# Second MoE of an attention + MoE + MoE kernel: the down side as seven block products, after a block's whole up side

## The chip, the cores and the metric

The kernel runs on one core of a Trainium2 chip. The core has five engines that the texts name as the profile does: PE (TensorE, matmuls; PEld is its weight loads), DVE (VectorE), ACT (ScalarE), POOL (GpSimd) and SP (SyncE, which here issues nearly all DMAs). Each engine runs its own instructions in order and waits on semaphores that the others raise. The metric is the device time of one execution in microseconds, lower is better.

## The reference

Attention with a memory term gives x of 2304 tokens x 512; two MoE-like layers follow, and only the second is touched here (cut to what matters):

```python
def _moe2_ref(x, w_gate, w_val, w_out):        # x 2304x512, d_ff 1536
    g = x @ w_gate
    silu = g * (1.0 / (1.0 + np.exp(-g)))
    val = x @ w_val
    return (silu * val @ w_out).astype(np.float32)

def reference(**kwargs):
    ...
    attn_out = _attn_ref(**attn_kwargs)
    x = attn_out.transpose(0, 2, 1, 3).reshape(B * S, H * D)
    x = _moe_ref(x=x, **moe_kwargs)            # the same without w_val, d_ff 2048
    return _moe2_ref(x=x, **moe2_kwargs)
```

All is float32. The kernel computes each float32 product as three products of a high and a low half (high x high, low x high, high x low) in the float32r format, so every logical matmul is three on PE.

## The kernel before, in words

One program, three stages that overlap. Attention and the first MoE run mixed: a generator (moe1) hands out pieces of the first MoE, and the main loop puts attention steps between them by a table of goals; Tile's scheduler then orders each engine by a model of times. The first MoE works in segments of 256 or 320 tokens: h = x W_in (line 824), tanh on ACT, a product on DVE, the halves gh on ACT and gl on POOL (line 834), y = g W_out (line 883). Its result goes to DRAM (yd).

**Preparing the second MoE's weights** (prep_w2) runs step by step beside that: a step every third yield of moe1 in attention (every=3), every fourth later (late=4). Per f-tile j (12 of 128 columns of d_ff) it loads and decodes the gate, value and down weights in turn, forms on POOL the sums that Strassen's products need of gate and value (S), splits all into halves (high on ACT, low on POOL) and writes them to DRAM, four tiles a j for the up side (wd2) and one for the down side (wdo, or directly the resident wos). By the end of the first MoE all is prepared; the down weights of all 12 f-tiles lie in SBUF (wos).

**The second MoE** takes 3 blocks i of 768 tokens. The up side computes gate and value of one f-tile for both halves of a block (384 tokens each) by Strassen's seven products in Winograd's form instead of eight: up(i, j) issues seven groups of six matmuls of 384 columns (2 pieces of the contraction x 3 halves) into four kinds of PSUM banks: a (product A11, later A12), c (S1), b (copied from a by ACT, then S2, S3, A22 on top) and d (added by DVE from b and c, then S4). Seven names of y (B11, T1, T2, B21, T3, B22, T4) are the sums of tokens that y_prep forms. Then tanh (ACT) and three DVE operations give the gated result r of each half.

The down side is a plain product: split_p splits a result r into ph (ACT, line 1174) and pl (POOL, line 1175); down adds, per f-tile and half, three token tiles x three matmuls of 512 columns into three resident banks po; after the twelfth f-tile ACT scales a bank into ot and SP writes it out. These nine matmuls are cut into three units, and up puts them between its own products: the down side of one half follows results that exist already, and the last half of the last block remains for the end.

In the second MoE the order of PE is the written one (manual_schedule); the other engines are ordered by the scheduler. stream() loads the four weight tiles of an f-tile one f-tile ahead, through eight buffers. y_prep of the next block runs at j = 8 to 11. The lines that make the chain between PE and the helpers:

```python
        nc.scalar.copy(b, a)                    # 1144
        product(b, "S2", "T2", False)
        d = seeded("d")
        nc.vector.tensor_add(d, b, e)           # 1147
```

## Time and profile before

| | before |
|---|---|
| three timed runs | 1105.01 us median (1103.02 to 1108.28) |
| the profiled execution's own time | 1105.75 us |
| its span on the core | 1103.9 us |
| PE busy / weight loads busy | 1070.8 us (97%) / 967.4 us (88%) |
| DVE, ACT, POOL busy | 609.2, 524.8, 453.2 us |
| DMA | 224.6 MB, 203 GB/s in the mean |
| chain that ended last | PE 77%, DVE 8%, DMA 7%, ACT 3%, POOL 3% |
| PE's share of that chain by line | 824: 14%, 1189: 14%, 883: 13%, 1120: 24% in all |

Busy time of PE counts the time in which at least one matmul is in flight, and the next one begins before the last one ends, so 97% does not say how dense the matmuls follow each other: that is read from starts. A row of a timeline merges neighbouring instructions of one kind: its start, how long it took from first start to last end, and, in brackets, the idle time of its engine before it and who ended it.

### The profile page before, as it was taken

The numbers are of one execution on the slowest core, as the hardware profiler recorded it, in microseconds if no ns is written. First come the engines' busy times: TensorE is split into PE (matmuls) and PEld (weight loads), VectorE is DVE, ScalarE is ACT, GpSimd is POOL, SyncE is SP. The second block draws the span as 40 slices with busy tenths as digits, with TensorE's granted clock in tenths as the row PEclk, the third lists the DMA queues.
The fourth block names the chain that finished last, engine by engine and source line by source line (L and its number), as shares of the span: only waits on it lengthen the run. The fifth ranks groups of instructions, "written<-read, shape, count | busy, mean of one in ns | idle before, by whom it ended". The sixth has DMA issues, their size and how long they took to land.

```text
span 1103.9 us, 19308 instructions
## 1 busy us (share of the span) xinstructions
PE 1070.8 (97%) x6899; PEld 967.4 (88%) x6899; DVE 609.2 (55%) x1412; ACT 524.8 (48%) x1261; POOL 453.2 (41%) x529
## 2 busy tenths in 40 slices
PE   7889999999999999999999999999999999999998
PEld 4566888888899889988899999999899999999986
DVE  6997588986566656466744564333643333333320
ACT  6665587765666465556644442222522323323222
POOL 3676446576666455656434831001211111121122
PEclk8987999999999999999999999999999999999999
DMA  8876576565688566785459866666654554655501
GB/s 212 280 213 208 158 241 207 155 206 172 216 286 268 198 193 212 274 293 182 150 209 391 287 251 228 202 194 192 237 183 159 182 172 142 201 162 177 175 20 49
DMA packets 155344, 224.64 MB, mean 203 GB/s; under 512 B 75632, under 2 KB 108400, under 8 KB 155248
## 3 DMA queue, kind: packets, MB, share of 16 engines
q1 hardware_dynamic: 153072, 223.00, 62.1%
q8 instruction: 55, 0.90, 0.3%
q10 hardware_dynamic: 2176, 0.40, 0.2%
q14 instruction: 41, 0.34, 0.1%
HBM read 169.88 MB, written 53.48 MB: 202 GB/s over the span
## 4 chain that ended last, share of the span: by engine, by line
PE 77%; DVE 8%; DMA 7%; ACT 3%; POOL 3%; issue 2%; SPq 0%; POOLq 0%; ACTq 0%; DVEq 0%
PE h L824 14%; PE po L1189 14%; PE y L883 13%; PE gb L1120 10%; PE ga L1120 7%; PE gd L1120 3%; PE gc L1120 3%; PE pss L403 3%; PE U L588 3%; PE pst L336 3%; DMA raw<-in_moe_w_out_dram 2%; DMA raw<-in_moe_w_val_dram 2%; DVE t L701 1%; PE psm L414 1%; PE pss L478 1%
## 5 line engine op out<-in xcount | busy, mean ns | idle before, releaser
L1175 POOL TENSOR_TENSOR pl<-r,ph 128x384 fp32r<-128x384 f32 x72 | 75.1, 1051 | 343.4 <-ACT ph L1174 282.2
L883 PE MATMUL y<-gh,w 128*128 128x320 f32 (+1 forms) x1024 | 175.2, 305 | 1.8 <-DVE th L832 1.5
L824 PE MATMUL h<-xh,w 128*128 128x320 f32 (+1 forms) x1024 | 171.3, 306 | 5.4 <-ACT w L209 2.3
L834 POOL TENSOR_TENSOR gl<-th,gh 128x256 fp32r<-128x256 f32 (+1 forms) x128 | 112.3, 881 | 131.2 <-ACT gh L209 97.0
L824 PEld LDWEIGHTS h<-xh,w 128*128 128x128 f32 x1024 | 146.1, 192 | 13.7 <-ACT w L209 3.7
L883 PEld LDWEIGHTS y<-gh,w 128*128 128x128 f32 x1024 | 146.8, 190 | 7.9 <-DVE th L832 2.5
L1189 PE MATMUL po<-wo,ph 128*128 128x512 f32 x432 | 133.8, 395 | 1.1 <-ACT ph L1174 0.7
L1120 PE MATMUL gb<-yT,w 128*128 128x384 f32 x648 | 131.7, 338 | 2.8 <-ACT gb L1144 1.4
L1120 PEld LDWEIGHTS gb<-yT,w 128*128 128x128 f32 x648 | 116.1, 188 | 12.7 <-ACT gb L1144 2.1
L1147 DVE TENSOR_TENSOR gd<-gb,e 128x384 f32<-128x384 f32 x36 | 20.4, 565 | 145.5 <-PE gb L1120 142.4
L832 DVE SCALAR_TENSOR_TENSOR th<-th,h 128x256 f32<-128x256 f32 (+1 forms) x128 | 56.9, 450 | 73.3 <-ACT th L831 73.0
L883 PE MATMUL y<-gl,w 128*128 128x320 f32 (+1 forms) x512 | 94.4, 300 | 0.2 <-POOL gl L834 0.2
L824 PE MATMUL h<-xl,w 128*128 128x320 f32 (+1 forms) x512 | 93.1, 301 | 0.0
L1189 PEld LDWEIGHTS po<-wo,ph 128*128 128x128 f32 x432 | 79.2, 188 | 9.7 <-ACT ph L1174 1.0
L1120 PE MATMUL ga<-yB,w 128*128 128x384 f32 x432 | 87.2, 337 | 0.0
L492 POOL TENSOR_TENSOR s<-s,r 128x128 f32<-128x128 f32 (+4 forms) x96 | 71.5, 771 | 37.8 <-DVE r L504 24.9
L1189 PE MATMUL po<-wo,pl 128*128 128x512 f32 x216 | 84.5, 399 | 0.7 <-POOL pl L1175 0.7
L459 ACT ACTIVATE s<-s,mn 128x128 f32<-128x128 f32 (+3 forms) x128 | 70.9, 555 | 22.9 <-DVE mn L455 22.2
L209 ACT CAST gh<-th 128x256 fp32r<-128x256 f32 (+1 forms) x128 | 54.6, 431 | 56.0 <-DVE th L832 35.3
L824 PEld LDWEIGHTS h<-xl,w 128*128 128x128 f32 x512 | 76.4, 191 | 2.5 <-issue 1.9
L1120 PEld LDWEIGHTS ga<-yB,w 128*128 128x128 f32 x432 | 76.8, 188 | 2.1
L1174 ACT CAST ph<-r 128x384 fp32r<-128x384 f32 x72 | 36.1, 513 | 89.0 <-PE po L1189 57.2
(142 smaller groups left out, 1975.7 us busy)
## 6 DMA issues: line engine op xcount, KB each, us to landing
w<-wg SPq DMA_DIRECT2D x108, 512.0 KB, 4.3
w<-wd SPq DMA_DIRECT2D x80, 512.0 KB, 4.9
wg<-wo SPq DMA_DIRECT2D x36, 512.0 KB, 3.6
wd<-w SPq DMA_DIRECT2D x32, 512.0 KB, 3.5
raw<-in_moe_w_out_dram SPq DMA_DIRECT2D x28, 512.0 KB, 4.6
wo<-wo SPq DMA_DIRECT2D x20, 512.0 KB, 5.7
w<-wg SPq DMA_DIRECT2D x36, 256.0 KB, 3.3
raw<-in_moe_w_in_dram SPq DMA_DIRECT2D x16, 512.0 KB, 5.5
```

What stands on the lines that cost most here:

```text
L209: nc.scalar.copy(out, in_)
L336: nc.tensor.matmul(dst, src, ident[0:n, 0:n], start=start, stop=True, is_transpose=True, skip_group_check=True)
L459: nc.scalar.activation(out=a, in_=a, func=ACTF.Exp, scale=-1.0, bias=mn, accum_out=o["sm", sup][:, col:col + 1])
L492: nc.gpsimd.tensor_mul(a, a, r.to_broadcast([P, w]))
L824: nc.tensor.matmul(ps[:, :nt], w[:, kk, :], x[:, kk, :nt], start=(m == 0), stop=(m == 3 * KD - 1))
L832: nc.vector.scalar_tensor_tensor(th[:, :nt], th[:, :nt], 1.0, ps[:, :nt], ALU.add, ALU.mult)
L834: tt(CFG["gl" if n >= CFG["n0"] else "gl0"]).tensor_sub(gl[:, :nt], th[:, :nt], f(gh[:, :nt]))
L883: nc.tensor.matmul(ps[:, :nt], w[:, c], g[:, :nt], start=(m == 0), stop=(m == last))
L1120: nc.tensor.matmul(dst, ws[nw][wi][:, P * kk:P * kk + P], y[ny][:, yi, kk], start=(start and m == 0), stop=(stop and m == 5), skip_group_c ...
L1174: nc.scalar.copy(ph, r)
L1175: nc.gpsimd.tensor_sub(pl, r, f(ph))
L1189: nc.tensor.matmul(po[t], a[:, c], w, start=(j == 0 and n == 0), stop=(j == F2 - 1 and n == 2))
```

## The change

- **Order of a block.** up is cut into its seven products, and a table (pe_order) sets the order of PE: product y of f-tile x stands at 7x + 2y, so the products of two neighbouring f-tiles alternate; the block's whole up side comes first, then its down side; the first three units of the down side stand between the last up products, and the last two between the first products of the next block.
- **Down side by seven products.** The block is seen as 2 x 2: token halves by f-tile parity on the one side, f-tile parity by the halves of the 512 output columns on the other. halved forms the sums of the results on POOL (and one on DVE, in split_p), and for each of seven products (DQ) and each of six pairs q of f-tiles nine matmuls of 256 columns add into a sum tile. Results of products are joined by a few ACT, DVE and POOL operations on 768 columns (snap, ot).
- **PSUM.** a and c share a tile of two banks; these tiles and the down side's sums are one pool of two tiles (ps_o); b and d have two banks each.
- **Weights.** prep_w2 first does gate and value of all f-tiles, then the down weights in pairs: four sums on POOL, then the splits, written to DRAM as seven pieces. Five of the seven are streamed through the same eight buffers in each block; two (S2, S4) are loaded once and stay. late=2: a step every second yield. Nothing of this remains for the second MoE.
- **Splits.** pl is formed by POOL, or for every other pair by DVE; the splits run six units ahead.
- y_prep keeps seven buffers, one a name; the factor of the output lies in the gating.

The core of the diff:

```diff
-    late=4,
+    late=2,
+    res='S2 S4',
...
-        todo = [(j, part) for j in range(F2) for part in range(3)]
+        todo = [(j, part) for j in range(F2) for part in range(2)] + [(j, 2) for j in range(F2)]
...
+        for q in range(NJ2):
+            g, x = divmod(q, 2)
...
+            e.tensor_sub(S[:, 0], a[:, 1], a[:, 0])
+            e.tensor_sub(S[:, 1], c[:, 1], S[:, 0])
+            e.tensor_sub(S[:, 2], c[:, 1], a[:, 1])
+            e.tensor_sub(S[:, 3], c[:, 0], S[:, 1])
+            halves(a[:, 0:1], 1, to("B11"))
+            halves(c, 2, to("B21"), to("B22"))
+            flush()
+            yield
+            halves(S[:, 0:2], 2, to("T1"), to("T2"))
+            halves(S[:, 2:4], 2, to("T3"), to("T4"))
+            yield paused()
...
+        ph2["o"] = ctx.enter_context(tc.tile_pool(name="ps_o", bufs=2, space=PSUM))
...
+            got += [(at + 2 * y + 7 * x, ("u", i, x, y)) for x in range(F2) for y in range(7)]
+            for n in range(len(DQ)):
+                for y in range(NJ2):
+                    k = n * NJ2 + y
+                    z = at + (end - 5 + 2 * k if k < 3 else end + k)
+                    if i + 1 < NB2 and k >= len(DQ) * NJ2 - 2:
+                        z = at + 1001 + 2 * (k - len(DQ) * NJ2 + 2)
+                    got.append((z, ("d", i, n, y)))
...
+    def stream(at):
+
+        while len(loaded) < len(loads):
+            n = len(loaded)
+            key = loads[n]
+            if n >= 2 * NW and last[loads[n - 2 * NW]] >= at or at < 0 and n >= NW:
+                return
...
+        if p == 0:
+            t = ph2["o"].tile([P, 1024], F32, tag="o", name="oac")
+            o["a"], o["c"] = t[:, 0:HT], t[:, 512:512 + HT]
+            product(o["a"], "A11", "B11", True)
+            o["b"] = seeded("b")
+            nc.scalar.copy(o["b"], o["a"])
...
+        elif p == 2:
+            product(o["b"], "S2", "T2", False)
+            o["d"] = seeded("d")
+            nc.vector.tensor_add(o["d"], o["b"], o["e"])
+        elif p == 3:
+            product(o["a"], "A12", "B21", False)
+            gated(0)
...
-        nc.scalar.copy(ph, r)
-        nc.gpsimd.tensor_sub(pl, r, f(ph))
...
+        nc.scalar.copy(ph, src)
+        (nc.gpsimd if n == 0 or q % 2 else nc.vector).tensor_sub(pl, src, f(ph))
         return ph, pl
 
+    def halved(i, q):
+
+        queue.append(split_p(i, 0, q))
+        a11, a21, a22 = pt[0, 2 * q], pt[1, 2 * q], pt[1, 2 * q + 1]
+        s1[q] = ph2["pr"].tile([P, HT], F32, tag=f"s{q}", name="s1")
+        nc.gpsimd.tensor_sub(a11, a11, a21)
+        nc.gpsimd.tensor_add(s1[q], a21, a22)
+        nc.gpsimd.tensor_sub(a21, a22, a11)
...
         for t in ts:
             c = slice(P * t, P * t + P)
-            for n, (a, w) in enumerate(((ph, wh), (ph, wl), (pl, wh))):
+            for m, (a, x) in enumerate(((ph, wh), (ph, wl), (pl, wh))):
                 nc.tensor.matmul(
-                    po[t], a[:, c], w, start=(j == 0 and n == 0), stop=(j == F2 - 1 and n == 2)
+                    g[1][:, 256 * t:256 * t + 256], a[:, c], x, start=(begin and m == 0 and t != 1),
+                    stop=(end and m == 2), skip_group_check=True,
                 )
...
+        G = {"A11": 0, "A12": 0, "S1": 1, "S4": 1, "S2": 2, "S3": 2, "A22": 3}[nm]
+        begin = q == 0 and nm in ("A11", "S1", "S2", "A22")
+        if begin:
+            acc[G] = ph2["o"].tile([P, 1024], F32, tag="o", name=f"po{G}")[:, 0:3 * 256]
...
+        if nm in ("A11", "S1"):
+            nc.scalar.copy(s, g)
+        elif nm == "A12":
+            ot, go = put_out(i, 0, 0)
+            nc.scalar.copy(ot, g)
+            go()
...
+            for t in range(HT // P):
+                for x, pr in late:
+                    piece_mm(nm, (i, g), x, pr, (t,), False, x == q)
+                c = slice(256 * t, 256 * t + 256)
+                nc.vector.tensor_add(ot[:, c], g[:, c], snap["x"][:, c])
+                go(range(t, t + 1))
```

Three places show what stands on an engine before and after. **PE in the up side** of the first block, first before: ga, gb, gc and gd are the banks a to d of one f-tile (the number tells the f-tile's tile), y names the sum of tokens, po the down side.

```order
L1120 MATMUL ga_9486<-yB11_8767,w_9388 128x384 x6
L1120 MATMUL gc_9493<-yT1_8771,w_9390 128x384 x6
L1189 MATMUL po_9416<-wo1_8125,ph_9482 128x512 x2
L1189 MATMUL po_9416<-wo1_8125,pl_9483 128x512
L1120 MATMUL gb_9505<-yT2_8795,w_9390 128x384 x6
L1120 MATMUL ga_9486<-yB21_8820,w_9388 128x384 x6
L1189 MATMUL po_9437<-wo1_8125,ph_9482 128x512 x2
```

The same place after; oac is the shared tile of a and c.

```order
L1171 MATMUL oac_9661<-yB11_8883,w_9585 128x384 x6
L1171 MATMUL gb_9600<-yT3_9066,w_9587 128x384 x6
L1171 MATMUL oac_9661<-yT1_8887,w_9589 128x384 x6
L1171 MATMUL gd_9634<-yB22_9137,w_9587 128x384 x6
L1171 MATMUL gb_9668<-yT2_8975,w_9589 128x384 x6
L1171 MATMUL gb_9600<-yT4_9141,w_9591 128x384 x6
```

Before, the products of one f-tile follow each other with a unit of the down side between some of them. After, no down unit stands there, and the bank gb_9668 of one f-tile is written between two products into gb_9600 of the one ahead of it.

**ACT at the end of product A12** of the first block, after the change (before has no such place; there ACT copies one bank of 512 columns after each half, line 1195). ph_10547 is a split for the product S2 that comes next, ot_10551 the copy of A12's sum; what each waits for stands in brackets.

```order
L1241 CAST ph_10534<-r_10058 128x384 [waits DVE_49,PE_49]
L1241 CAST ph_10547<-r_10202 128x384 [waits PE_49,Pool_49]
L1316 COPY ot_10551<-po0_10237 128x768 [waits PE_49]
L1241 CAST ph_10571<-r_9566 128x384 [waits DVE_49,PE_49]
L1241 CAST ph_10585<-r_9710 128x384 [waits PE_49,Pool_49]
```

The copy of the sum stands behind the last cast for S2 and ahead of the casts for S4.

**POOL behind attention,** first before: gl is the low half that the first MoE waits for, wo a low half of prepared weights, raw8 a mark that lets the next load start.

```order
L834 TENSOR_TENSOR gl_7895<-th_7893,gh_7894 128x256
L834 TENSOR_TENSOR gl_8028<-th_8026,gh_8027 128x256
L834 TENSOR_TENSOR gl_8048<-th_8046,gh_8047 128x256
L683 COPY raw8_8053<-gl_8028 128x1
L683 COPY raw8_8061<-gl_8028 128x1
L683 COPY raw8_8064<-gl_8028 128x1
L834 TENSOR_TENSOR gl_8082<-th_8080,gh_8081 128x320
L834 TENSOR_TENSOR gl_8104<-th_8102,gh_8103 128x320
```

After, some segments on; S2 holds the sums of a pair of down weights.

```order
L998 TENSOR_TENSOR S2_8341<-t2_8247 128x256
L1000 TENSOR_TENSOR S2_8341<-t2_8301,t2_8247 128x256
L684 COPY raw8_8442<-gl_8408 128x1
L999 TENSOR_TENSOR S2_8341<-t2_8301,S2_8341 128x256
L835 TENSOR_TENSOR gl_8428<-th_8426,gh_8427 128x256
L1001 TENSOR_TENSOR S2_8341<-t2_8301,S2_8341 128x256
L952 TENSOR_TENSOR wo_8346<-t2_8247,wo_8346 128x256
L835 TENSOR_TENSOR gl_8460<-th_8458,gh_8459 128x320
L952 TENSOR_TENSOR wo_8349<-t2_8301,wo_8349 128x2x256
```

There the sums and splits of the down weights now stand between the gl subtractions of the first MoE, five times.

## Rows read from the trace of the kernel before

**Rows 1.** The page: busy time by engine, and TensorE's granted clock in 40 slices.

```profile
PE 1070.8 (97%) x6899; PEld 967.4 (88%) x6899; DVE 609.2 (55%) x1412; ACT 524.8 (48%) x1261; POOL 453.2 (41%) x529
...
PEclk8987999999999999999999999999999999999999
```

**Rows 2.** Windows by stage: busy us and instructions of each engine, clock, DMA.

```profile
230.00:570.00 340.00, 333.49 (x2532) 304.24 (x2531) 216.84 (x576) 204.37 (x521) 199.49 (x252) 1.00 0.66 217
570.00:679.00 109.00, 107.70 (x798) 107.20 (x798) 56.91 (x94) 44.35 (x98) 50.38 (x56) 1.00 0.80 289
...
679.00:1100.40 421.40, 416.76 (x2158) 384.05 (x2156) 149.13 (x232) 122.15 (x244) 75.07 (x72) 1.00 0.52 169
...
600.00:640.00 40.00, 38.70 (x291) 38.30 (x290) 22.23 (x37) 17.99 (x41) 29.91 (x32) 1.00 0.89 312
```

**Rows 3.** Timeline of PE, 256 columns: start us, us, line, shape, count.

```profile
663.46 1.12 PE L883 MATMUL y<-gh,w 128*128 128x256 f32 x8
...
664.90 1.12 PE L883 MATMUL y<-gh,w 128*128 128x256 f32 x8
```

**Rows 4.** Timeline of PE, 384 columns, in the up side.

```profile
684.46 1.20 PE L1120 MATMUL gd<-yB,w 128*128 128x384 f32 x6
...
686.54 1.20 PE L1120 MATMUL ga<-yB,w 128*128 128x384 f32 x6
```

**Rows 5.** Timeline of PE, 512 columns, the end of the down side.

```profile
1098.09 0.63 PE L1189 MATMUL po<-wo,ph 128*128 128x512 f32 x2
...
1099.96 0.39 PE L1189 MATMUL po<-wo,pl 128*128 128x512 f32 x1
```

**Rows 6.** Groups by form: count | busy us, mean ns | idle us before, releasers.

```profile
L1189 PE MATMUL po<-wo,ph 128*128 128x512 f32 x432 | 133.8, 395 | 1.1 <-ACT ph L1174 0.7 <-ACT ot L1195 0.5
...
L1189 PE MATMUL po<-wo,pl 128*128 128x512 f32 x216 | 84.5, 399 | 0.7 <-POOL pl L1175 0.7
...
L1189 PEld LDWEIGHTS po<-wo,ph 128*128 128x128 f32 x432 | 79.2, 188 | 9.7 <-ACT ph L1174 1.0 <-ACT ot L1195 0.9
```

**Rows 7.** Timeline of PE from 679: the longest waits, in brackets with releaser.

```profile
681.05 1.32 PE L1120 MATMUL gb<-yT,w 128*128 128x384 f32 x6 [0.83 <-ACT gb L1144]
...
794.53 0.74 PE L1189 MATMUL po<-wo,ph 128*128 128x512 f32 x2 [0.67 <-ACT ph L1174]
...
800.64 1.32 PE L1120 MATMUL gb<-yT,w 128*128 128x384 f32 x6 [1.38 <-DVE gd L1147]
...
1074.89 0.74 PE L1189 MATMUL po<-wo,ph 128*128 128x512 f32 x2 [0.45 <-ACT ot L1195]
```

**Rows 8.** Durations of DVE's add, ACT's copy (groups) and casts (timeline).

```profile
L1147 DVE TENSOR_TENSOR gd<-gb,e 128x384 f32<-128x384 f32 x36 | 20.4, 565 | 145.5 <-PE gb L1120 142.4 <-PE gd L1130 3.1
...
L1195 ACT ACTIVATE ot<-po 128x512 f32<-128x512 f32 x18 | 10.6, 596 | 10.4 <-PE po L1189 8.8 <-DMA out_dram<-ot 1.6
...
1070.92 1.79 ACT L1174 CAST ph<-r 128x384 fp32r<-128x384 f32 x4 [1.89 <-DVE r L1165]
```

**Rows 9.** The page, DMA issues: count, KB each, us to landing.

```profile
w<-wg SPq DMA_DIRECT2D x108, 512.0 KB, 4.3
```

**Rows 10.** Timeline at the end of a block: DVE alone, POOL, DVE beside POOL.

```profile
793.12 0.95 DVE L1010 TENSOR_TENSOR yB<-ytop,yB 128x768 fp32r<-128x768 f32 x1
...
794.55 6.41 POOL L1175 TENSOR_TENSOR pl<-r,ph 128x384 fp32r<-128x384 f32 x4 [9.97 <-ACT ph L1174]
...
798.35 1.77 DVE L1027 TENSOR_TENSOR yt<-ybot,ytop 128x768 f32<-128x768 f32 x1
```

**Rows 11.** Timeline in the first MoE: POOL's sum and split, PE's wait.

```profile
606.67 0.73 POOL L963 TENSOR_TENSOR S<-S,t 128x256 f32<-128x256 f32 x1
...
609.30 1.27 POOL L952 TENSOR_TENSOR wo<-S,wo 128x512 fp32r<-128x512 f32 x1
...
610.85 1.44 PE L824 MATMUL h<-xh,w 128*128 128x320 f32 x8 [1.00 <-DVE th L832]
```

**Rows 12.** Timeline of ACT: the last operation ahead of the last write.

```profile
1100.43 0.60 ACT L1195 ACTIVATE ot<-po 128x512 f32<-128x512 f32 x1 [1.54 <-PE po L1189]
```

More of the change, by code (lines that the diff above doesn't have):

```diff
@@ L914 @@
     NB2 = NT // T2
+    NJ2 = F2 // 2
     wd2, wdo = {}, {}
     PIECES = ("A11", "A12", "S1", "S2", "S3", "S4", "A22")
+    BQ = ("B11", "T1", "B21", "T2", "B22", "T3", "T4")
+    DQ = ("A11", "S1", "A12", "S2", "S4", "S3", "A22")
     def hl(t, n):
@@ new lines, with needs @@
+    pos = pe_order()
+    BW = dict(zip(DQ, BQ))
+    first, last = {}, {}
+    def needs():
+        for n, (kind, i, x, y) in enumerate(pos):
+            if kind == "u":
+                key = ("u", i, x, (0, 1, 1, 0, 2, 2, 3)[y])
+            elif DQ[x] not in RES:
+                key = ("d", i, x, y // 2)
+            else:
+                continue
+            first.setdefault(key, n)
+            last[key] = n
+    needs()
+    loads = sorted(first, key=first.get)
+    loaded, streamed = [], {}
@@ L1136, in up @@
-        product(a, "A11", "B11", True)
-        c = sum_bank("c", "gc")[:, :HT]
-        product(c, "S1", "T1", True)
-        e = ph2["tp"].tile([P, HT], F32, tag="e", name="e", bufs=2)
-        nc.scalar.copy(e, c)
-        if units:
-            units.pop(0)()
-        b = seeded("b")
-        nc.scalar.copy(b, a)
-        product(b, "S2", "T2", False)
-        d = seeded("d")
-        nc.vector.tensor_add(d, b, e)
-        product(a, "A12", "B21", False)
-        if units:
-            units.pop(0)()
@@ new lines, with split_p @@
+    pt, s1, queue, split = {}, {}, [], [0]
+    def split_p(i, n, q):
+        nm = DQ[n]
+        a11, a12, a21, a22 = pt[0, 2 * q], pt[0, 2 * q + 1], pt[1, 2 * q], pt[1, 2 * q + 1]
+        if nm == "S4":
+            nc.vector.tensor_sub(a12, a12, a21)
+        src = dict(A11=a11, S1=s1.get(q), A12=a12, S2=a21, S4=a12, S3=a11, A22=a22)[nm]
+        ph = ph2["pp"].tile([P, HT], F32R, tag="ph", name="ph", bufs=NJ2)
+        pl = ph2["pp"].tile([P, HT], F32R, tag="pl", name="pl", bufs=NJ2)
+        nc.scalar.copy(ph, src)
+        (nc.gpsimd if n == 0 or q % 2 else nc.vector).tensor_sub(pl, src, f(ph))
+        return ph, pl
@@ L1199 @@
+    late = []
     if True:
```

315 lines of the change are left out of this document (168 added, 147 removed).

## The prediction, made before the changed kernel was run

> **What bounds the kernel now.** I read the page's line on TensorE first: PE is busy 97% of a span of 1103.9 us, and its granted clock is 0.9 or more from the fifth of the forty slices on [rows 1]. So I ask of each stage how much of its time is matmuls at their own pace and how much is waiting. The windows by stage give the frame [rows 2]: attention beside the first MoE to 570 us, the first MoE alone to 679 us, the second MoE to 1100.4 us. In the last one no helper works half of the time (DVE 149, ACT 122, POOL 75 of 421.4 us).
>
> Pace is read from starts in the timeline, since one matmul's duration overlaps the next. Matmuls of 256 columns, each with a weight load of its own: 12 from 663.46 to 664.90 (8 in the first row, 4 in the one left out), 120 ns [rows 3]. Of 384 columns: 12 from 684.46 to 686.54, 173.3 ns [rows 4]. Of 512 columns on the down side: 8 from 1098.09 to 1099.96, 233.75 ns [rows 5]. At 2.4 GHz (granted clock 1.00 in these windows, rows 2) the columns alone take 106.7, 160 and 213.3 ns, so a matmul costs 13.3 ns above its columns at 256 and 384, and 20.4 at 512.
>
> The second MoE then adds up: 1,506 matmuls of up products (6 of the 1,512 run before 679) and 3 seeds at 173.3 ns are 261.5 us; 648 down matmuls [rows 6] at 233.75 ns are 151.5; together 413.0 of 421.4 us. The remaining 8.4 us are waits; the longest four [rows 7] are 3.3 us of them.
>
> **The sum, part by part**, against the profiled run's own 1105.75 us (its span and 1.8 around it; 0.7 above the median of 1105.01).
>
> *Down side.* Before: 3 blocks x 2 halves x 12 f-tiles x 3 token tiles x 3 = 648 matmuls of 512 columns. After: 3 blocks x 7 products x 6 pairs x 3 token tiles x 3 = 1,134 of 256. Columns fall by 12.5%, matmuls rise by 75%, so the result hangs on the cost per matmul. At the 120 ns of rows 3 it is 136.1 us: 15.4 less. The trace has no 256-column matmul on the down side; the bounds are 120 ns and 106.7 + 20.4 = 127.1 ns, if the larger overhead belongs to that side and not to 512 columns. I take 120: that row too has a load for every matmul, a full stationary operand and an output of part of a bank, whereas the 512-column ones read their moving operand in two separate halves and fill a bank. The high bound adds 8.1 us.
>
> *Up side.* 1,512 matmuls stay, and one seed more: +0.2 us. With two f-tiles alternating, every chain (product A11, ACT's copy into b, product S2, DVE's add, product S3) has two or three foreign products of 1.04 us between its links, where a copy or an add takes at most 0.6 us [rows 8]. DVE's six operations per f-tile are about 3.4 us of 7.3. This removes the waits on ACT and DVE in the course of the stage, but these are few.
>
> *Weights.* In the up stage 1.84 MB per f-tile now come in 7.3 us instead of 11.5: 252 GB/s, where 570 to 679 already ran at 289 with PE busy 107.7 of 109 us [rows 2]. By the rule in stream, SP issues four loads together some seven products (7.3 us) ahead of the first use, and such a load lands 4.3 us after its issue [rows 9]. I cost this at nothing; without that cover it would show as loads or matmuls that wait for DMA.
>
> *New waits.* The PSUM pool of the sums has two tiles of two banks. A12's sum must be copied out by ACT before S2 may start in the same tile, and the order of ACT puts one cast for S2, which itself waits for A12's last matmul, ahead of that copy. Everything of PE is queued behind S2's first matmul. Price: a cast 0.43 (four in 1.79 us, so 0.43 from start to start), the copy of 768 columns about 0.85 (0.596 for 512, at most half as much again) [rows 8], drain and signals about 0.25: 1.5 us each, bounds 1.0 and 2.0, three blocks, 4.5 us. From S4 to A22, the other such pair, six units of work lie between: nothing.
>
> At the end of the first two up stages DVE gets, in its order, nine operations of the next block's y and three splits among the last results. Alone they fit; where POOL works at the same time a DVE operation of 768 columns takes 1.77 instead of 0.95 us, and four splits of POOL 6.4 us [rows 10]. S1's last split waits for these results, then for two or three POOL operations. I take 1.0 us a time, 2.0 in all, bounds 0 and 8. At the very end token tile 1 shares a bank with tile 0, which DVE must first have read: 0.7 us (an add of 256 columns, under the 0.565 of 384 in rows 8, and signals). Of the waits that are spread thin I keep 1.9. New waits 9.1 against 8.4: +0.7 us.
>
> *Before the second MoE.* All matmuls there stay. The sums of the down weights go to POOL: for each of 6 pairs four sums of 0.73, three splits of 1.27 and one of half size [rows 11], 7.5 us, in place of two splits of 1.27. Gate and value weights go first, so five of the six pairs come after 570: five chains of 7.5 us beside the gl subtractions that PE waits for. POOL holds this: it was busy 50.4 of 109 us there [rows 2], and three chains more make it some 72. But in 600 to 640, where before has two such chains, PE was idle 1.3 us [rows 2, 11]. Five chains instead of two add about 2 us; the other order of attention from some 230 us on can go either way. +2, bounds -3 and +6.
>
> *End.* The last piece is a DVE add of 256 columns (about 0.4) for ACT's 0.60 [rows 12], and half the bytes: -0.3 us.
>
> Sum: -15.4 + 0.2 + 0.7 + 2.0 - 0.3 = -12.8, so **1093 us**, 1.2% below the profiled run and 1.1% below the median.
>
> **Rivals.** *The new waits stay hidden* (no hand-off, POOL no worse): 1093 - 4.5 - 2.0, about 1086. For it: few waits before; against: the hand-off stands in ACT's order. Chance 0.10.
>
> *The down side costs 127 ns a matmul:* +8.1, 1101, about the same as before. For it: every down matmul before shows 20 ns; against: those of 256 and 384 columns show 13 [rows 3, 4]. 0.12.
>
> *POOL's chains hold up the first MoE* (the slower side). POOL works in order; a gl behind a whole chain comes 7.5 us late, and with 3 us of slack PE loses 4.5 us a pair. Six pairs: 27 less the 2 in the sum, 1118. It decides from 2.9 us a pair on (17.5 us over the forecast passes the bound). For it: the wait of 1.0 us at 610.85 [rows 11]; against: the order sets gl between the pieces of a chain. 0.06.
>
> *Weight loads are not hidden,* so that the gain on paper isn't had at all. A load takes 188 ns [rows 6]; 486 more of them in the open are 91 us, 1093 + 91 = 1184. Against it: 120 ns from start to start hold a whole load and 107 ns of columns [rows 3], which leaves no room. 0.02. The Trainium skill, TensorE: Matmul & The Clock Gate (section "The mechanism", what overlaps and what doesn't), has LDWEIGHTS overlap matmuls in flight only where the row group differs; with its section "LDWEIGHTS (loading the stationary operand)", 486 more loads of 107 ns would be an estimate of 52 us on the path. By that rule the change loses; the row disagrees with it.
>
> **How the numbers follow.** Forecast 0.70 (1087 to 1100), the others 0.10, 0.12, 0.06, 0.02. Range 1084 to 1103.5: the first two rivals lie inside it. 0.5% (5.5 us) is about what a measurement of this kernel can tell from no change. Faster by more: 0.70 + 0.10 = 0.80; within: 0.12; slower: 0.06 + 0.02 = 0.08.
>
> **What would show it.** Right: about 120 ns between starts of down matmuls; 173 in the up stage; PE idle before S2 three times by 1 to 2 us, released by ACT's copy; nothing of PE waiting for DMA; the second MoE about 408 us from first to last product, the stages before it ending within some us of 679. Wrong: 127 ns or more; DVE or POOL ending PE's idle time in the down stage; waits on gl or th after 570 that add up to more than 5 us; a second MoE that starts much later.

## The result and the profile after

| | before | after |
|---|---|---|
| median of the first four runs each | 1104.01 us (1102.70 to 1108.28) | 1094.53 us (1093.63 to 1095.11) |
| ratio, 95% interval | | 0.9907 (0.9877 to 0.9936) |
| once more: 8 runs after, 19 before (run e11) | 1103.33 us | 1095.98 us (1091.73 to 1101.25) |
| ratio, 95% interval | | 0.9941 (0.9921 to 0.9962) |
| profiled execution, span | 1103.9 us | 1092.9 us |
| second MoE, from its first product behind the first MoE to the start of its last matmul | 421.1 us | 409.5 us |

The change makes the kernel faster, by 6.5 to 10.3 us by the two ratios, where 12 were forecast. The page after: PE is about as full as before (96% against 97%), with more matmuls, and POOL and DVE work more. These lines answer to [rows 1].

```profile
PE 1051.0 (96%) x7386; PEld 981.4 (90%) x7386; DVE 659.4 (60%) x1498; ACT 554.8 (51%) x1318; POOL 553.0 (51%) x622
...
PEclk8889999999999999999999999999999999999999
```

Windows by stage, with the columns of [rows 2] (PE, PEld, DVE, ACT, POOL busy; clock, DMA share, GB/s). The last row answers to 679.00:1100.40 there.

```profile
230.00:570.00 340.00, 330.88 (x2523) 303.76 (x2522) 206.78 (x557) 202.59 (x515) 205.09 (x259) 0.99 0.64 207
570.00:679.80 109.80, 106.80 (x781) 104.97 (x780) 64.58 (x101) 49.57 (x109) 73.91 (x83) 1.00 0.92 331
679.80:1089.40 409.60, 401.08 (x2652) 399.19 (x2650) 198.19 (x323) 148.10 (x293) 144.07 (x129) 1.00 0.69 236
```

The timeline of PE in the down side, every third row: start, us, line, tile, shape, count; between two of these starts lie three matmuls. It answers to [rows 3, 5].

```profile
783.96 0.28 PE L1263 MATMUL po<-w,pl 128*128 128x256 f32 x1
...
784.32 0.28 PE L1263 MATMUL po<-w,pl 128*128 128x256 f32 x1
...
785.40 0.28 PE L1263 MATMUL po<-w,pl 128*128 128x256 f32 x1
```

From 783.96 to 785.40 there are 12 matmuls in 1.44 us: **120.0 ns each**; 1,134 of them are 136.1 us. The up side keeps 173.3 ns (12 matmuls from 684.16 to 686.24). What remains is waiting. These are all waits of PE over 0.6 us in the second MoE, in brackets the idle time with its releaser. From the start of the matmul before the wait to the start of the one behind it, less the pace of one matmul, they cost 0.76, 1.54, 1.96, three times 1.40 and twice 0.68 us (the bracket is shorter, since it begins where the last matmul ends). Counted by its matmuls the third, at 789.88, is the fifth pair of A12, which waits for DVE's split:

```profile
681.79 1.32 PE L1171 MATMUL oac<-yT,w 128*128 128x384 f32 x6 [0.60 <-ACT gb L1205]
...
688.99 1.29 PE L1171 MATMUL oac<-yT,w 128*128 128x384 f32 x6 [1.38 <-DMA w<-wg]
...
789.88 0.38 PE L1263 MATMUL po<-w,pl 128*128 128x256 f32 x1 [1.80 <-DVE pl L1242]
...
793.28 0.50 PE L1263 MATMUL po<-resS,ph 128*128 128x256 f32 x2 [1.24 <-ACT ot L1316]
...
927.57 0.51 PE L1263 MATMUL po<-resS,ph 128*128 128x256 f32 x2 [1.24 <-ACT ot L1316]
...
1061.84 0.50 PE L1263 MATMUL po<-resS,ph 128*128 128x256 f32 x2 [1.24 <-ACT ot L1316]
...
1086.38 0.50 PE L1263 MATMUL po<-w,ph 128*128 128x256 f32 x2 [0.52 <-DVE ot L1300]
...
1088.22 0.50 PE L1263 MATMUL po<-w,ph 128*128 128x256 f32 x2 [0.52 <-DVE ot L1300]
```

The three waits of 1.40 us stand at the first matmul of S2. On ACT, the cast for S2 and then the copy of A12's sum stand ahead of the one at 793.28, and PE starts 0.05 us after the copy has ended:

```profile
792.02 0.51 ACT L1241 CAST ph<-r 128x384 fp32r<-128x384 f32 x1 [0.62 <-PE po L1263]
792.44 0.79 ACT L1316 COPY ot<-po 128x768 f32<-128x768 f32 x1
```

**The first MoE alone** waits at two places over 0.3 us (in brackets), and at both a helper works in its order. At 574.75 PE waits 1.22 us for yp, because DVE stood at the first operation of the token sums (y_prep), whose load had not landed, and yp is queued behind it:

```profile
572.38 0.96 DVE L1036 TENSOR_TENSOR yt<-ytop 128x768 f32<-128x768 f32 x1 [4.06 <-DMA ytop<-yd]
573.33 0.96 DVE L1030 TENSOR_TENSOR yB<-ytop,yB 128x768 fp32r<-128x768 f32 x1
574.21 0.49 DVE L889 SCALAR_TENSOR_TENSOR yp<-y,yp 128x320 f32<-128x320 f32 x1
```

At 614.78 it waits 1.68 us for gl, which stands on POOL behind three sums of a pair of down weights:

```profile
610.91 1.19 POOL L998 TENSOR_TENSOR S<-t 128x256 f32<-128x256 f32 x1
612.06 1.19 POOL L1000 TENSOR_TENSOR S<-t,t 128x256 f32<-128x256 f32 x1
613.18 0.19 POOL L684 COPY raw<-gl 128x1 f32<-128x1 f32 x1
613.32 0.73 POOL L999 TENSOR_TENSOR S<-t,S 128x256 f32<-128x256 f32 x1
614.00 0.73 POOL L835 TENSOR_TENSOR gl<-th,gh 128x256 fp32r<-128x256 f32 x1
```

**A start that differs by chance.** Up to 230 us all these kernels have the same instructions of PE in the same order, and yet the profile of before is 3.3 us behind there. The granted clock goes with it: from 80 to 116 us before had 0.81, after 1.00.

```profile
80.00:116.00 36.00, 34.31 (x205) 24.20 (x204) 23.54 (x60) 16.66 (x41) 18.03 (x17) 0.81 0.63 187
```

```profile
80.00:116.00 36.00, 33.38 (x243) 25.64 (x242) 25.60 (x64) 17.38 (x44) 19.29 (x17) 1.00 0.71 202
```

The first row is of before, the second of after: 38 fewer matmuls begin in the same 36 us. In the table below the profiles with 0.81 are at their first mark at 229.5 to 229.9 us, those with 1.00 at 224.8 to 226.5. So I compare stages, and take from each profile the time at which PE has begun 20%, 75% and 100% of the first MoE's matmul columns:

| profile | clock 80 to 116 | 20% at | 20% to 75% | 75% to 100% | second MoE, first to last | span |
|---|---|---|---|---|---|---|
| before | 0.81 | 229.8 | 343.7 | 105.2 | 421.1 | 1103.9 |
| after | 1.00 | 226.5 | 345.7 | 107.5 | 409.5 | 1092.9 |
| e11 (after again) | 1.00 | 224.8 | 347.7 | 107.5 | 411.1 | 1094.8 |
| e1 | 1.00 | 225.6 | 344.7 | 107.7 | 413.6 | 1095.3 |
| e2 | 0.81 | 229.9 | 346.7 | 107.6 | 439.2 | 1127.1 |
| e3 | 1.00 | 225.2 | 344.0 | 108.5 | 407.9 | 1089.7 |
| e4 | 0.81 | 229.8 | 344.6 | 111.5 | 410.2 | 1099.8 |
| e5 (before, other layout of weights) | 0.91 | 227.7 | 344.7 | 105.2 | 421.2 | 1102.9 |
| e6 | 1.00 | 226.4 | 344.5 | 109.7 | 415.8 | 1100.5 |
| e7 | 0.81 | 229.8 | 344.6 | 107.4 | 406.0 | 1091.6 |
| e8 | 1.00 | 225.0 | 355.3 | 103.4 | 409.3 | 1097.1 |
| e9 | 0.91 | 228.1 | 345.4 | 107.5 | 405.1 | 1090.1 |
| e10 | 0.81 | 229.8 | 347.2 | 109.4 | 414.4 | 1104.7 |
| e12 | 0.81 | 229.5 | 358.5 | 104.7 | 403.2 | 1100.4 |

Before and e5 run six up matmuls (1.04 us) in the last part of the first MoE, so that their 105.2 are 104.2 of its own. From 20% to 75%, beside attention, before and e5 have the same order and differ by 1.0 us; the profiles with the order of after lie at 344.5 to 347.7. A difference of 2 us there is thus not clear of chance. The 3.3 us behind it are there in every profile that keeps the order of after to the end of that stretch (107.4 to 107.7).

### The profile page after: what moved, and what is told of

It reads as the page before. It is cut to its first block, busy times and chain, and to the rows that moved or that the text cites. A ratio compares the mean times of both kernels' runs of the same rounds, so it can differ in the third digit from the quotient of the medians.

```text
span 1092.9 us, 20747 instructions
## 1 busy us (share of the span) xinstructions
PE 1051.0 (96%) x7386; PEld 981.4 (90%) x7386; DVE 659.4 (60%) x1498; ACT 554.8 (51%) x1318; POOL 553.0 (51%) x622
## 4 chain that ended last, share of the span: by engine, by line
PE 68%; DVE 10%; DMA 7%; POOL 5%; issue 4%; ACT 2%; SPq 0%; POOLq 0%; ACTq 0%; DVEq 0%
PE h L825 12%; PE y L884 12%; PE po L1263 11%; PE oac L1171 10%; PE gb L1171 10%; PE gd L1171 3%; PE U L589 3%; PE pss L404 2%; PE pst L337 2%; DMA raw<-in_moe_w_val_dram 2%; POOL gl L835 1%; DMA raw<-in_moe_w_gate_dram 1%; DMA w<-wg 1%; POOL s L493 1%; DVE raw L702 1%
## 5 line engine op out<-in xcount | busy, mean ns | idle before, releaser
L825 PE MATMUL h<-xh,w 128*128 128x256 f32 (+1 forms) x1024 | 170.7, 305 | 7.3 <-ACT w L210 3.2
L1242 POOL TENSOR_TENSOR pl<-r,ph 128x384 fp32r<-128x384 f32 x63 | 69.1, 1100 | 199.4 <-ACT ph L1241 179.9
L1171 PE MATMUL gb<-yT,w 128*128 128x384 f32 x648 | 124.8, 336 | 0.0
L1263 PE MATMUL po<-w,ph 128*128 128x256 f32 x540 | 98.2, 283 | 1.0 <-DVE ot L1300 1.0
L1241 ACT CAST ph<-r 128x384 fp32r<-128x384 f32 x108 | 55.0, 513 | 85.1 <-PE po L1263 45.7
L1263 PEld LDWEIGHTS po<-w,ph 128*128 128x128 f32 x540 | 84.9, 191 | 1.4 <-DVE ot L1300 1.4
L1171 PE MATMUL oac<-yB,w 128*128 128x384 f32 x432 | 81.3, 336 | 0.0
L884 PEld LDWEIGHTS y<-gl,w 128*128 128x128 f32 x512 | 76.6, 191 | 2.5 <-POOL gl L835 2.2
L1263 PE MATMUL po<-w,pl 128*128 128x256 f32 x270 | 76.4, 283 | 1.8 <-DVE pl L1242 1.8
L1171 PEld LDWEIGHTS oac<-yB,w 128*128 128x128 f32 x432 | 75.4, 188 | 0.0
```

The source lines that it names most:

```text
L825: nc.tensor.matmul(ps[:, :nt], w[:, kk, :], x[:, kk, :nt], start=(m == 0), stop=(m == 3 * KD - 1))
L884: nc.tensor.matmul(ps[:, :nt], w[:, c], g[:, :nt], start=(m == 0), stop=(m == last))
L1171: nc.tensor.matmul(dst, w[wi][:, P * kk:P * kk + P], y[ny][:, yi, kk], start=(start and m == 0), stop=(stop and m == 5), skip_group_check= ...
L1241: nc.scalar.copy(ph, src)
L1242: (nc.gpsimd if n == 0 or q % 2 else nc.vector).tensor_sub(pl, src, f(ph))
L1263: nc.tensor.matmul(g[1][:, 256 * t:256 * t + 256], a[:, c], x, start=(begin and m == 0 and t != 1), stop=(end and m == 2), skip_group_chec ...
```

## Experiments

**e1: product S4 ahead of S2**, so that the copy of A12's sum has six units of time.

```diff
-    DQ = ("A11", "S1", "A12", "S2", "S4", "S3", "A22")
+    DQ = ("A11", "S1", "A12", "S4", "S2", "S3", "A22")
...
         elif nm == "S4":
             ot, go = put_out(i, 0, 1)
-            nc.vector.tensor_add(ot, g, snap["x"])
-            go()
+            nc.vector.tensor_add(ot, g, snap["u1"])
+            held.append((ot, go))
```

> Product S4 goes ahead of S2 in the down side, so that six units of work (6.5 us) lie between the last matmul of A12 and the first one that writes into A12's sum tile again; S4 and A22 still have six units between them. One more DVE operation of 768 columns per block. Theory (the three waits of 1.40 us are the hand-off of one PSUM tile by ACT's copy): all three vanish, 4.2 us less, 1094.5 -> about 1090.3. Rival (the copy only hides that the splits of the next product are late): PE waits at the same three places on DVE's or ACT's splits, S4's sooner needed subtractions above all, by 1 us or more each, and the time stays at 1094.

Measured: 1098.84 us, ratio 0.996 (0.9942 to 0.9978); second MoE 413.6. The three waits of 1.40 are gone, and a wait of 2.12 us (1.96 in the bracket) stands three times at another place, at S3's first matmul. Neither theory had it:

```profile
802.35 0.96 DVE L1320 TENSOR_TENSOR snap<-po,snap 128x768 f32<-128x768 f32 x1
803.22 0.95 DVE L1322 TENSOR_TENSOR ot<-po,ot 128x768 f32<-128x768 f32 x1
```

```profile
804.27 0.47 PE L1264 MATMUL po<-w,ph 128*128 128x256 f32 x2 [1.96 <-issue]
```

In the new order S3 follows S2 at once, both add into one tile, and two DVE operations read it between. PE starts 0.10 us after the second has ended, so I take DVE as the releaser, though the row names none. The swap removed one hand-off and made a dearer one, which I had overlooked: three times 2.12 less 1.40 is 2.2 us more, and e1's ratio lies 0.2% over that of e11, though the two intervals overlap. The mechanism holds; the cure was wrong.

**e7: S2 and S3 in other banks.** The sum goes into three banks that the up side leaves free; the products keep their order.

```diff
-            acc[G] = ph2["o"].tile([P, 1024], F32, tag="o", name=f"po{G}")[:, 0:3 * 256]
+            if G == 2:
+                acc[G] = [sum_bank(x, "po2")[:, 0:256] for x in "bbd"]
+            else:
+                acc[G] = ph2["o"].tile([P, 1024], F32, tag="o", name=f"po{G}")[:, 0:3 * 256]
```

> The sum of S2 and S3 goes into three of the four banks that the up side's b and d leave free in the down side; the order of the products is that of the changed kernel. S2 then starts in banks that nothing reads, six units still lie between S2's last matmul and S3's first, and A22 takes the tile that A12's copy has left long before. Theory (a product waits for whoever still reads its sum tile, and for nothing else): the three waits of 1.40 us go and none comes in their place, 4.2 us less of waits in the second MoE. Rival (splits are late as well): PE waits at S2 on DVE or ACT for 0.5 us or more each time.

Measured, by one profile: second MoE 406.0 us, and none of the three waits, nor another in their place; in the down sides of the three blocks only DVE's split in A12 (1.96, first block) and the two at the end are left. Three times 1.40 is 4.2; the second MoE gained 3.5 against after and 5.0 against e11. These are no clean measure of the 4.2: the wait for a weight load is 0.53 us shorter than in after, and behind the split's wait e7 had a clock of 0.57 from 792 to 796 us where after had 1.00 (the last section comes back to this). e7 does not compute the same sums: read from the code, which begins products of 256 columns in banks where the up side adds 384 onto what ACT or DVE put there ahead, the sums b and d of the later blocks lose a part of it; no run followed this. The work on PE is the same in number and shape.

**e2: no alternation.**

```diff
-            got += [(at + 2 * y + 7 * x, ("u", i, x, y)) for x in range(F2) for y in range(7)]
+            got += [(at + y + 7 * x, ("u", i, x, y)) for x in range(F2) for y in range(7)]
```

> One number in the order of PE: product y of f-tile x stands at 7x + y and not at 7x + 2y, so that the seven products of an f-tile follow each other with nothing between them; all else as in the changed kernel. Theory (the two foreign products between the links are the cover): each f-tile shows the wait that the very first one shows now, S1 behind ACT's copy of A11's sum in the same tile, 0.77 us, 35 times more: 27 us, about 1121. Rival (the chain has cover enough in its own products, as in the kernel before, where such waits were few): 1094 to 1098.

Measured, by one profile: 1128.87 us; second MoE 439.2, 29.7 more than after. Every f-tile but the first of the second and third block shows the wait, 0.72 to 0.80 us from start to start:

```profile
727.42 1.31 PE L1171 MATMUL oac<-yT,w 128*128 128x384 f32 x6 [0.55 <-ACT gb L1205]
...
735.54 1.31 PE L1171 MATMUL oac<-yT,w 128*128 128x384 f32 x6 [0.55 <-ACT gb L1205]
...
743.65 1.31 PE L1171 MATMUL oac<-yT,w 128*128 128x384 f32 x6 [0.55 <-ACT gb L1205]
```

That is 34 waits; the 33 that after does not have make 24.2 us, and the matmul behind each starts 0.11 us late, 3.6 us more. At the ends of the first two up stages DVE, busy with the token sums, adds 2.2 us each; against that, A12's 1.96 and the load's 1.54 are gone. The theory held, and 1121 was 8 us too low. The alternation is what carries the shared tile of a and c.

**e3 and e4: POOL's sums of the down weights** left out (T1 to T4 then hold other numbers), or given to DVE.

```diff
-            e.tensor_sub(S[:, 0], a[:, 1], a[:, 0])
-            e.tensor_sub(S[:, 1], c[:, 1], S[:, 0])
-            e.tensor_sub(S[:, 2], c[:, 1], a[:, 1])
-            e.tensor_sub(S[:, 3], c[:, 0], S[:, 1])
...
-            halves(S[:, 0:2], 2, to("T1"), to("T2"))
-            halves(S[:, 2:4], 2, to("T3"), to("T4"))
```

> Leaves out the four sums of each pair of down weights and their two splits (T1 to T4 hold other numbers; the writes and their bytes stay): 4 x 0.73 + 2 x 1.27 = 5.5 of POOL's 7.5 us a pair, and two ACT casts. Theory (POOL's chains are a part of what the first MoE lost): the wait of 1.7 us on gl at 614.8 goes, the 1.2 us at 574.7 on DVE stays, the stretch from 570 to the first product of the second MoE falls from 109.8 to about 107.5: 1092.5. Rival one (chains of POOL are the whole loss of attention and first MoE, 5.3 us from 230 on): 1089. Rival two (they cost nothing; the order of attention and the first block's token sums do): 1094.5, with the stretch at 109 to 110.

> The four sums of each pair of down weights go from POOL to DVE, which is busy 64.6 of 109.8 us there; POOL keeps the splits, 4.6 us a pair instead of 7.5. Theory (POOL's chains cost about 2 us): half of what leaving them out gives, the wait on gl shorter than 1.7 us, 1093.5. Rival (DVE, which PE waits for through th and yp, gets worse): waits on DVE th and yp grow by more than 1 us, 1096.

Measured: e3 1094.74 us, ratio 0.9938 (0.9904 to 0.9971), the last quarter of the first MoE 108.5 us, 1.0 more than after; e4 1099.47, 0.9964 (0.9939 to 0.9989), that quarter 111.5. In e3 the wait on gl of 1.68 is gone, and others stand there:

```profile
580.70 1.17 PE L884 MATMUL y<-gh,w 128*128 128x256 f32 x6 [1.26 <-DVE th L833]
597.60 0.42 PE L884 MATMUL y<-gl,w 128*128 128x320 f32 x1 [0.77 <-POOL gl L835]
619.41 0.99 PE L884 MATMUL y<-gh,w 128*128 128x320 f32 x5 [0.94 <-ACT gh L210]
636.09 0.86 PE L884 MATMUL y<-gh,w 128*128 128x256 f32 x5 [1.07 <-ACT gh L210]
```

So POOL's chains alone are not the price, since with 5.5 of their 7.5 us gone nothing is gained; the second rival of e3 stands as far as it speaks of POOL. For e4 its rival came true in part: PE waits for DVE's th (1.43 us, in brackets) and for ACT's gh (2.87), which it had not named, while the wait on yp stays (1.15 against 1.22).

**e8: no preparing of the down weights at all**; copies of a gate weight's piece fill the DRAM tiles.

```diff
-            halves(a[:, 0:1], 1, to("B11"))
-            halves(c, 2, to("B21"), to("B22"))
-            flush()
...
+            for d in BQ:
+                nc.sync.dma_start(out=to(d), in_=wd2[0][0][:, 0:2])
```

> Leaves out the preparing of the down weights altogether (loads, decoding, sums, splits on ACT, DVE and POOL); the pieces in DRAM are filled with copies of a gate weight's piece, so the second MoE's work is unchanged. Theory (the preparing that now falls behind attention costs what the first MoE lost, whichever engine shows it): the columns done by 570 us to the end of the first MoE take 1 to 2 us less than in the changed kernel's profile, waits of PE there 1.2 us (yp) instead of 2.9. Rival (the token sums of the first block and the order of attention cost it): waits stay at about 3 us.

Measured, by one profile: the last quarter takes 103.4 us, 4.1 less than after, where 1 to 2 were put, and 0.8 less than before's own 104.2; the waits of 1.22 and 1.68 us are gone, and the largest left, in brackets, are 0.22 us at 591.93 and 0.58 for yp at 684.57. This fits that what the first MoE lost, 3.3 us, is the price of the preparing that falls there, whichever engine shows it. It does not prove it: the part beside attention became 9.6 us longer than after, in another order of PE and of the helpers from some 250 us on, so that the helpers came to the last quarter with more time. Why that part became longer stays open, and no net gain was seen.

**e12: the same work beside attention instead** (on top of e9, below).

```diff
-    every=3,
+    every=2,
```

> e9 with one number changed: a step of preparing the second MoE's weights at every second piece of the first MoE already beside attention (every=2, as it is after attention), where e9 takes every third. Some 69 instead of 46 steps then lie beside attention, and nearly none behind it. Theory (what the first MoE alone loses, 3.3 us against the kernel before, is the price of the preparing that falls there, whoever shows the wait): the stretch from 570 on loses as little as in e8, 3 to 4 us less than e9; attention has spare time on every engine, so it pays at most 2 us: 1088 to 1090 where e9 has 1091.4. Rival (steps beside attention cost PE as much there, by POOL and DVE in order): attention ends 3 us or more later, 1091 to 1095.

Measured: 1099.32 us, ratio 0.9946 (0.9912 to 0.9980), where e9 has 0.9888. The last quarter falls by 2.8 us (107.5 to 104.7), near the 3 to 4 of the theory, but the part beside attention takes 13.1 us more (345.4 to 358.5), against 2 at most. That is the rival's direction, at four times its size. Beside attention POOL is busy 245.7 of 340 us there, in e9 205.6:

```profile
230.00:570.00 340.00, 325.49 (x2425) 295.17 (x2426) 229.47 (x574) 210.38 (x532) 245.72 (x305) 0.99 0.74 249
```

**e5: the kernel before, down weights in one run of 512** columns for each half.

```diff
-            hi, lo = hl(w, n)
+            hi, lo = (r_(w[:, 0:2]), r_(w[:, 2:4])) if apart else hl(w, n)
...
-        wh, wl = (r_(wos[j].rearrange("p (k h) n -> p h k n", h=2)[:, x]) for x in range(2))
+        wh, wl = (r_(wos[j].rearrange("p (h k) n -> p h (k n)", h=2)[:, x]) for x in range(2))
```

> The kernel before; in the resident down weights the two high pieces of 256 columns lie next to each other and the two low ones too, so that a 512-column matmul reads one run of 512 values and not two runs of 256 with a gap. Same matmuls, same bytes. Theory of the prediction (the 20.4 us-thousandths above the columns at 512 come from the operand read in two pieces, and the down side at 256 columns pays 13.3): 648 down matmuls go from 233.75 to about 226.6 ns from start to start, 4.6 us less, second MoE about 417 us. Rival (the full bank, or 512 columns as such): 233.75 stays, and the cost of a matmul above its columns grows with the width.

(The "20.4 us-thousandths" are 20.4 ns.) Measured, by one profile: 1104.73 us, second MoE 421.2; the pace is unchanged:

```profile
1096.13 0.40 PE L1189 MATMUL po<-wo,pl 128*128 128x512 f32 x1
...
1098.23 0.40 PE L1189 MATMUL po<-wo,pl 128*128 128x512 f32 x1
```

Nine matmuls in 2.10 us are 233.3 ns. The two separate halves, which the prediction gave as a reason for the 20.4 ns, are not the cause. That the output fills a bank, or the width as such, remains and was not told apart.

**e6: four small edits**, each at a place of its own.

```diff
+            if tail:
+                acc[G] = [acc[G][:, 0:256], sum_bank("b", "pob")[:, 0:256], sum_bank("d", "pod")[:, 0:256]]
...
+            nc.gpsimd.tensor_copy(r_(res[nm][:, 4 * g, 0:1]), pt[1, 3][:, 0:1])
             nc.sync.dma_start(out=res[nm][:, 4 * g:4 * g + 4], in_=wdo[BW[nm], g])
...
-    y0=32,
+    y0=16,
...
+        if i:
+            for x in (top, bot):
+                nc.scalar.copy(x[:, 0, 0:1], snap["u1"][:, 0:1])
```

> The changed kernel with four small edits, each seen at a place of its own: the last product's three token tiles in three PSUM banks of different tiles; the six resident weight loads wait for a result of f-tile 3; the token sums of the first block half as early (y0=16); the loads for the next blocks' token sums wait for the copy of A11's sum, so that DVE's burst comes after the splits of S1. Theory: both waits of 0.68 us in the last 7 us go; the wait for a weight load at 689 (1.54 us) goes; the wait of 1.0 to 1.4 us on yp at 573 to 579 goes; the wait on DVE's split at 790 (1.96 us) goes or falls under 0.5. Together up to 6.5 us, 1088 from the same start. Rivals: the tiles share nothing and the tail's waits are DVE's own time (0.68 stays); the weight load is late because of the queue's bytes and not of the six loads ahead of it; the burst turns up before A12's or S2's units with the same 2 us.

Measured, by one profile: 1102.34 us. The two waits at the end are gone, so token tiles in different banks of one tile do wait for each other's readers, and in separate tiles do not. The wait for a weight load at 689 is gone, with one of 0.47 at 732 in its place. The wait on yp stays (1.08 at 573.39). And the burst of the token sums came back at A12's copy, as its rival says, and in both blocks (the expectations here and of e10 put the wait at 790 in S1; it is A12's fifth pair):

```profile
794.45 0.79 PE L1268 MATMUL po<-resS,ph 128*128 128x256 f32 x2 [3.95 <-ACT ot L1324]
```

```profile
934.19 0.79 PE L1268 MATMUL po<-resS,ph 128*128 128x256 f32 x2 [4.49 <-ACT ot L1324]
```

ACT had casts of 768 columns for the token sums (0.83 us each) in its order ahead of that copy: 4.1 and 4.65 us instead of 1.40.

**e11, the changed kernel again; e9, three edits joined; e10, e9 with the burst later.** In e9 the banks of S2 and S3 are filled by ACT with A11's sum and go on accumulating, and e6's first two edits are in it.

```diff
             nc.scalar.copy(s, g)
+            if nm == "A11":
+                acc[2] = [sum_bank(x, "po2")[:, 0:256] for x in "bbd"]
+                for t in range(3):
+                    nc.scalar.copy(acc[2][t], s[:, 256 * t:256 * t + 256])
```

> The changed kernel itself, once more, beside the kernel before on the same chip. All profiles so far have the same order of instructions to about 230 us, and yet reach its end (the same matmul) between 225.0 and 229.9 us; so single spans carry up to 4.9 us of that. From equal starts the profiles of before and after differ by 7.7 us (second MoE and end 13.0 less, what lies between 230 and the second MoE 5.3 more). If that is the change's worth, the ratio of many runs is about 0.993 (8 us, 1095.5 where before has 1103.3). If the medians of the first four runs each are right, 0.991 (9.5 us). The second MoE's eight waits over 0.6 us come again within 0.1 us each, since its order is fixed; those of the first MoE (yp, gl) too.

> The changed kernel with three edits: S2 and S3 add into three free banks of the up side, which ACT fills with the copy of A11's sum ahead of it, so that the banks' columns go on accumulating as they stand and the later sum needs no add; the last product's three token tiles in banks of different tiles; the resident weight loads wait for a result of f-tile 3. Theory (each wait of PE in the second MoE is a hand-off of one tile or a load behind others): three waits of 1.40 us, two of 0.68 go, that for a weight load falls from 1.54 to 0.5: 6.6 us less from the first to the last product, 409.5 -> 403, and about 1088.5 where the changed kernel has 1095. Rival (the copies on ACT, 1.2 us a block, delay the casts): PE waits on ACT's ph in S1 or A12 by more than 1 us a block; then 1091 or more.

> e9 and, as in e6, the loads for the next block's token sums wait for the copy of A11's sum. In e6 this moved the burst of the token sums from DVE at S1 (1.96 us once) to ACT at A12 (4.1 and 4.65 us, 5.95 more than the hand-off alone). With S2 in banks of its own nobody waits for A12's copy. Theory (only the hand-off made that burst costly): the 1.96 us goes and nothing comes: 2 us less than e9, 1086.5. Rival (ACT's seven copies of 768 columns a block also stand ahead of the casts that S2 needs): PE waits on ACT's ph at S2 or S4, 2 us or more in each of the first two blocks, 1090 or more.

Measured: e11 1095.98 us, 0.9941 (0.9921 to 0.9962), as put from equal starts (0.993) and not as the first medians (0.991). Its waits are after's, but for the weight load (0.81 instead of 1.54) and yp in the first MoE (1.00 instead of 1.22 in brackets), and its second MoE is 1.6 us longer. **e9: 1091.43 us, ratio to before 0.9888 (0.9866 to 0.9909)**, 4.5 us under e11, the best of all: the hand-offs and the end's waits are gone, and the load's wait is 1.02 at 731.55. That load and DVE's 1.95 in A12 are what is left over 0.8. Of the 6.6 us expected the second MoE shows 6.0 against e11 and 4.4 against after; the time, 4.5 by the medians or 5.8 by the ratios. e10: 1102.54, 1.0004 (0.9989 to 1.0019): the burst goes from A12 to S2, third and fifth pair. The rival is right on place and sign, but the releaser is DVE, not ACT, and it is dearer than put:

```profile
800.45 0.39 PE L1272 MATMUL po<-resS,pl 128*128 128x256 f32 x1 [1.49 <-DVE pl L1246]
806.02 0.58 PE L1272 MATMUL po<-resS,pl 128*128 128x256 f32 x1 [3.16 <-DVE pl L1246]
```

The same pair stands in the second block, some 10 us in all. The last quarter of the first MoE, too, takes 2 us more than in e9 (109.4 against 107.5), as in e6 (109.7): both have another order from some 600 us on, and what of the edit brought that, I have not followed. DVE's work for the next block's tokens has to be done once a block somewhere; early in the down side, where it stood in after, it cost 2 us once.

## Why the prediction was right, and where it was off

The time lies in the range and the sign holds. By its terms:

| term | forecast | measured |
|---|---|---|
| down side, 1,134 x 120 against 648 x 233.75 ns | -15.4 | -15.4 |
| seed | +0.2 | +0.2 |
| waits of the second MoE | +0.7 (9.1 against 8.4) | +2.4 (10.7 against 8.3) |
| from 230 us to the second MoE | +2.0 | +5.3 (2.0 in attention, 3.3 behind it) |
| end | -0.3 | -0.3 |
| sum | -12.8 | -7.8 |

The forecast of 1093 was nearer to the first median of 1094.5 than its terms deserve: the start was 3.3 us ahead in the one profile, and the ratio of more runs is 0.9941, where 1093 of 1105.01 is 0.989. What the terms add up to, 7.8 us, lies between the two measured differences (6.5 and 10.3 us by their ratios). So the mechanism of the gain was right, and that 1093 came within 1.5 us of the first median is in part luck. In the waits of the second MoE, too, errors cancel in part: the end, the weight load and the first f-tile's wait cost 3.0 us more than put, the waits spread thin 1.0 us less.

- **Cost of a down matmul:** right, 120.0 against the rival's 127. One reason given for it, that the operand in two separate halves costs the 20 ns at 512 columns, is refuted by e5.
- **Weight loads:** right. Every down matmul has a load, and these take 191 ns each in the trace, as before; at 120 ns from start to start they cannot all be on the path. The Trainium skill, TensorE: Matmul & The Clock Gate (section "The mechanism"), has LDWEIGHTS overlap matmuls in flight only where the row group differs; these rows, all of 128x128, disagree, 120.0 ns with a load each. The same section also lets a load for a background weight buffer run ahead of matmuls, which these rows would fit.

```profile
L1263 PEld LDWEIGHTS po<-w,ph 128*128 128x128 f32 x540 | 84.9, 191 | 1.4 <-DVE ot L1300 1.4
```

- **Hand-off of A12's tile:** right in place, releaser and size: 1.40 three times, forecast 1.5 (of which the 0.25 for drain and signals came from no row); e7 and e9 take it away and nothing follows.
- **Burst of the token sums:** the cause is right, DVE's queue; the place is one product later (A12's fifth pair, not S1's last), 1.96 us once and not 1.0 twice. In the second block the wait is under 0.1 us.
- **End:** I priced one wait of 0.7 for a shared bank; there are two of 0.68, since also the third token tile, which shares no bank with its neighbour, waits for the reader of their common tile (e6).
- **Weights "at nothing":** off by 0.8 to 1.5 us. The six loads of the resident pieces, whose place on SP I had not looked at, go ahead of the streamed ones; held back, the wait shrinks and moves (e6, e9).
- **Before the second MoE:** the term that failed. I priced POOL's sums alone, from before's two chains. The 3.3 us behind attention are there in every profile with that order (75% to 100%: 107.4 to 107.7 us in after, e1, e2, e7, e9, e11, against 105.2 with the six up matmuls in before and e5), and after's waits on yp and gl, 1.38 and 1.84 us from start to start, are as much. But e3 shows that without the sums others are late, and in e8, without the preparing, the stretch loses nothing. The step that failed is "five chains instead of two add about 2 us": it counted one engine's operations, where a step of preparing has loads, decoding on ACT and DVE, sums and splits. That the preparing as a whole is the price fits e8 and e12 but was not isolated, since in both the part beside attention became longer. The 2.0 us in attention are within what profiles of one order differ by. The move of the first block's token sums was not priced at all (the 1.22 us). The upper bound of +6 did hold. (The rival's threshold of 2.9 us a pair leaves out the 2 us that the sum already holds; with them it is 3.3.)
- **The rival of 1086,** waits hidden, was not the case here, but its first half is what e9 makes of the kernel.

## What to carry over

Price a step of work that is moved by every engine and queue that it uses, and then ask which of them stands ahead of something that PE needs; here, taking one engine's share away only changed who was late. In this kernel a PSUM tile is handed over when its last reader is done: before two products are exchanged, list for each tile who reads it between its uses, since the reader that waited before may only be the first of two. And where differences of some us matter, compare stages between the same instructions in several profiles: the start alone differed by 5 us here.

## What the hardware showed that I had not expected

**The clock adds to a wait, and not every time.** At the wait of 1.96 us in the first block's A12 after kept its clock; in e11, the same program, the waits at 789 and 793 are the same within 0.04 us, and the granted clock was at half for some microseconds. The windows of after, then of e11:

```profile
793.00:796.00 3.00, 2.71 (x22) 2.72 (x23) 0.56 (x1) 1.07 (x3) 0.61 (x1) 1.00 0.88 305
```

```profile
793.00:796.00 3.00, 2.58 (x12) 2.58 (x13) 0.00 (x0) 0.84 (x2) 0.74 (x1) 0.50 0.86 298
796.00:800.00 4.00, 4.00 (x29) 4.00 (x29) 1.12 (x2) 1.28 (x4) 1.02 (x1) 0.80 0.02 6
```

At 1.2 instead of 2.4 GHz 12 matmuls start where 22 did: about 2 us more than the wait itself. e11's second MoE has 1.6 us over after's although its weight load waits 0.73 less. After the split's wait of 1.79 us alone (in brackets) it fell too in e9, whose window follows, and in e7 (0.57):

```profile
792.00:796.00 4.00, 4.00 (x23) 4.00 (x23) 1.87 (x4) 1.95 (x4) 1.00 (x1) 0.58 0.21 78
```

At the start it is the same. PE's wait at 84 us took 1.85 us in before and 1.27 in after, and from 90 to 100 us before had 0.54, after 1.00; but in e1 and e8 that wait is as long as in before, and there too the clock was 1.00. So the length of such a wait does not decide it. It cost here its own length or some 2 us more, and removing one can be worth more than a good profile shows.

**DVE beside POOL.** A split of 384 columns on DVE takes 0.55 us at the least and 1.37 at the most (median 0.56):

```profile
L1242 DVE TENSOR_TENSOR pl<-r,ph x45: 545/559/1370, 781.2 to 1080.9; 128x384 fp32r<-128x384 f32 x45
```

All that take over 0.6 us overlap an operation of POOL, as from 777 to 786 us; two that overlap one nearly throughout stay short. It is a part of what makes the burst of the token sums hold up A12: the split that ends the wait at 789.88 took 1.34 us. The Trainium skill has it in SBUF — State Buffer (section "SBUF: two separate sides"): the port pair that DVE and GpSimd share is an exclusive lock, and the one that comes second is blocked. The trace agrees as far as the slowing goes, 1.37 against 0.56; that it is a lock, no row here shows.
